# Two heads' first 64 queries in one softmax block: an attention and MoE kernel on one Trainium2 core

## Chip, core and metric

The kernel runs on one core of one Trainium2 chip. The metric is the time of one execution in device microseconds, taken as the median of several runs. TensorE is called PE here, VectorE DVE, ScalarE ACT, GpSimd POOL; SP is the engine that issues most DMAs. PEld is PE's loading of weights.

## What is computed

Causal attention over 2 batches, 12 heads, 448 positions, head size 64, and behind it two feed-forward parts:

```python
scores = scale * np.matmul(q, k.transpose(0, 1, 3, 2))
scores = np.where(mask, -1000000000.0, scores)       # mask: strictly above the diagonal
scores = scores - np.max(scores, axis=-1, keepdims=True)
attn = np.exp(scores)
attn = attn / (np.sum(attn, axis=-1, keepdims=True) + 1e-09)
x = np.matmul(attn, v)                               # then heads side by side: 896 x 768
h = (x @ w1) * (x @ w2) @ w3 @ w_out
r = np.maximum(h @ w_in2, 0.0)
out = (r * r) @ w_out2
```

## The kernel before

**Pairs and blocks.** The 24 heads are handled as 12 pairs; the two heads of a pair lie on partitions 0 to 63 and 64 to 127 of one tile `qk`. The 448 queries of a head are cut into four blocks of 128 rows (NCH = 4). Block i sees WIDTH[i] = 64 + 128 i keys: 64, 192, 320 and 448. Block 0 holds the first 64 queries on its upper 64 partitions; its lower 64 rows are the last 64 queries of the rolled tensor, carried along and never used. SHORT = 64 is that first width.

**One pair's steps.** `scores` (L668) has PE multiply queries by keys, for both heads in turn, into tiles `s`, two blocks to a tile in the order (3, 0), (2, 1). `minimum` (L709) has DVE apply the mask, write the block to tile `p` and take the row's extreme into `st`; each is followed by a short read of the accumulator. `softmax` (L715) has ACT exponentiate a block and sum its rows, DVE add 1e-9 and take reciprocals of four sums (`reciprocals`, L727, one call for each head), and DVE multiply each block by them. Then PE transposes: `short_transposes` (L763, tile `ph`) the blocks of 64 columns, eight for a pair, and `transposes` (L742, tile `pp`) the full ones. ACT copies both into `pt_all`; `attend` (L788, tile `x`) multiplies by the values, and `x_parts` splits the result for the products behind it.

**What lies between.** PE also forms w3 @ w_out during attention, in pieces called `w` (`fill`, `w_half`). From pair 4 on, one loop of the main program puts on PE: scores of pair p, `ph` of pair p-1, one `w`, the `pp`, two `w`, `x`. In the first loops PE does the scores of pairs 0 and 1, then 32 transposes of a constant (`warm`, L841), then `ph` of pair 0. From about 151 us on, PE works on the feed-forward products (tiles `bank`).

**Who sets the order.** Every step is entered in a `Program` (L28) with its engines, a cost on each and the places it reads and writes. PE's steps keep the order in which they are entered. For DVE, ACT and SP a list planner (`Program.order`, L59) works out due times backwards from PE's steps and gives each engine the ready step that is due first. The order is then fixed; each engine runs its list in order.

```python
mm(s_t[p, j, g][:, o:o + w], y[own, 0, rows_of(i):rows_of(i) + P], y[own, 1, :w], True, True)
prog.add({"V": (300, 380)}, reciprocals, sums, sums)
nc.tensor.transpose(x[0][:SHORT, o:o + SHORT], block(p, j, c)[SHORT:, c * P:c * P + SHORT], ident[SHORT:, SHORT:])
```

Of the kernel before, what the change touches and what calls it, by code (L numbers as in the profile page):

```python
# [8 lines left out]
F32 = mybir.dt.float32  # L9
F32R = mybir.dt.float32r  # L10
U32 = mybir.dt.uint32
AF = mybir.ActivationFunctionType
# [112 lines left out]
def attention_moe_moe2(ctx: ExitStack, tc: tile.TileContext, qk, v, w1, w2, w3, w_out, w_in2, w_out2, out):  # L125
# [48 lines left out]
    def mm(o, l, r, start, stop, **more):  # L174
        return nc.tensor.matmul(o, l, r, start=start, stop=stop, **more)  # L175
# [138 lines left out]
    for g in range(N3 // KF):  # L314
# [16 lines left out]
    wraw = [attw.tile([P, DM], F32, tag=f"W{i}", name=f"wraw{i}") for i in range(KF)]  # L331
    ident = attc.tile([P, P], F32, tag="ident", name="ident")
    mask = attc.tile([P, S], F32, tag="mask", name="mask")
    pt_all = attc.tile([P, 3, NCH * (SHORT + S) // 2], F32, tag="pt", name="pt_all")
    make_identity(nc, ident)
    nc.gpsimd.memset(mask, 0.0)
# [1 line left out]
        out=mask, in_=mask, compare_op=ALU.is_ge, fill=MASKED,  # L338
        base=S - P, pattern=[[-1, S]], channel_multiplier=1,
    )  # L340


    prog = Program({"S": 700, "V": 700})
# [319 lines left out]
        prog.add({"S": (700, 2900)}, run, [], [("v", p % 2)], turn="v")  # L663

    def place_p(p, j, i):
        return "p", (2 * p + j) % 4, i

    def scores(p):  # L668
        def open_tiles():
            st_t[p] = att.tile([P, 4, 2, NCH], F32, tag="st", name=f"st{p}", bufs=3)  # L670
            for h in (2 * p, 2 * p + 1):
                p_t[h] = att.tile([P, off[NCH]], F32, tag="p", name=f"p{h}", bufs=4)

        at = {}
        for g in BLOCKS:
            for j in range(2):
                at[j, g] = turn("a", 6)
        for g in BLOCKS:
            o = 0
            for i in g:  # L680
                w = WIDTH[i]

                def run(e, g=g, i=i, o=o, w=w):
                    if g == BLOCKS[0]:
# [8 lines left out]
                opened = [place_p(p, j, i2) for j in range(2) for i2 in range(NCH)] if g == BLOCKS[0] else []  # L693
                a = 3.3 if p == 0 and i == BLOCKS[0][0] else 1.856
                prog.add({"T": (a * w, a * w + 250)}, run, [("qk", p % 3)],
                         [("a", at[j, g]) for j in range(2)] + opened)
                o += w
        for j in range(2):
            for g in BLOCKS:
                o = 0  # L700
                for i in g:
                    w = WIDTH[i]
                    minimum(p, j, g, i, o, w, at[j, g])
                    o += w

    def block(p, j, i):
        return p_t[2 * p + j][:, off[i]:off[i + 1]]

    def minimum(p, j, g, i, o, w, place):  # L709
        gap = 80 + 1.031 * w  # L710
        prog.add({"V": (gap, gap + 160)}, lambda e: nc.vector.tensor_tensor_reduce(  # L711
            block(p, j, i), s_t[p, j, g][:, o:o + w], mask[:, S - w:], QS, 3.0e38,
            ALU.add, ALU.min, st_t[p][:, 0, j, i:i + 1]), [("a", place)], [place_p(p, j, i), ("st", p % 3, j, i)])

    def softmax(p, j):  # L715
        sums = []
        for g in BLOCKS:
            for i in g:
                w = WIDTH[i]
                gap = 272 + 0.882 * w  # L720
                prog.add({"A": (gap, gap + 100)}, lambda e, i=i: nc.scalar.activation(  # L721
                    block(p, j, i), block(p, j, i), AF.Exp, bias=st_t[p][:, 0, j, i:i + 1], scale=-1.0,
                    accum_out=st_t[p][:, 1, j, i:i + 1]),
                    [place_p(p, j, i), ("st", p % 3, j, i)], [place_p(p, j, i), ("st", p % 3, j, i)])
                sums.append(("st", p % 3, j, i))
# [6 lines left out]
        prog.add({"V": (300, 380)}, reciprocals, sums, sums)  # L732
        for g in BLOCKS:
            for i in g:
                w = WIDTH[i]
                on_v = 70 + 0.67 * w
                prog.add({"V": (on_v, on_v + 85)},
                         lambda e, i=i: nc.vector.tensor_scalar(  # L738
                             block(p, j, i), block(p, j, i), st_t[p][:, 3, j, i:i + 1], None, ALU.mult),
                         [place_p(p, j, i), ("st", p % 3, j, i)], [place_p(p, j, i)])  # L740

    def transposes(h):  # L742
        p, j = divmod(h, 2)
# [19 lines left out]
    def short_transposes(p):  # L763
        x, place = [], turn("a", 6)

        def run(e):
            x.append(ps_a.tile([P, S + SHORT], F32, tag="a", name=f"ph{p}"))
            for j in range(2):
                for c in range(NCH):
                    o = (j * NCH + HALF_AT[c]) * SHORT  # L770
                    nc.tensor.transpose(x[0][:SHORT, o:o + SHORT], block(p, j, c)[SHORT:, c * P:c * P + SHORT],
                                        ident[SHORT:, SHORT:])

        t = 2 * NCH * 56
        prog.add({"T": (t, t + 160)}, run, [place_p(p, j, i) for j in range(2) for i in range(NCH)], [("a", place)])
        for j in range(2):
            h = 2 * p + j

            for c, d in ((0, 1), (3, 2)):
                def out(e, j=j, h=h, c=c, d=d):  # L780
                    src = x[0][:SHORT, j * NCH * SHORT:(j + 1) * NCH * SHORT].rearrange("p (n c) -> p n c", c=SHORT)
# [682 lines left out]
```

## Time and profile before

| What | us |
|---|---|
| Median of 3 runs | 518.12 (516.83 to 518.4) |
| The profiled execution | 518.19 |
| its span, first to last instruction | 516.4 |
| DVE busy in the span | 478.6 |
| ACT busy in the span | 396.8 |

The profiled execution takes 1.8 us more than its span; that part lies around the instructions. Its granted clock is 0.999 of full speed. Times in the rows below count from the start of the span. A busy PE says little by itself: its matmuls are pipelined, the start of one lies before the end of the last, and their ends are modelled. The distance from start to start is what a matmul costs.

### The profile page before, as it was taken

The numbers are of one execution on the slowest core, as the hardware profiler recorded it, in microseconds if no ns is written. First come the engines' busy times: TensorE is split into PE (matmuls) and PEld (weight loads), VectorE is DVE, ScalarE is ACT, GpSimd is POOL, SyncE is SP. The second block draws the span as 40 slices with busy tenths as digits, with TensorE's granted clock in tenths as the row PEclk, the third lists the DMA queues.
The fourth block names the chain that finished last, engine by engine and source line by source line (L and its number), as shares of the span: only waits on it lengthen the run. The fifth ranks groups of instructions, "written<-read, shape, count | busy, mean of one in ns | idle before, by whom it ended". The sixth has DMA issues, their size and how long they took to land.

```text
span 516.4 us, 8564 instructions
## 1 busy us (share of the span) xinstructions
PE 510.5 (99%) x2915; PEld 464.5 (90%) x2915; DVE 478.6 (93%) x1147; ACT 396.8 (77%) x979; POOL 16.2 (3%) x24
## 2 busy tenths in 40 slices
PE   9999999999999999999999999999999999999997
PEld 7668888888889999999999999999999999999997
DVE  4999999999969999997976899999999999999994
ACT  5998999767859574638486479998999698969870
POOL 1000000000000012121100000000000000000000
PEclk9999999999999999999999999999999999999999
DMA  8955555563242887999754301505520642061014
GB/s 312 330 199 219 200 176 182 181 225 142 83 157 105 282 233 185 304 179 296 158 151 152 123 0 56 190 1 214 204 72 1 237 161 94 0 241 65 2 62 154
DMA packets 27340, 81.69 MB, mean 158 GB/s; under 512 B 2464, under 2 KB 13472, under 8 KB 27296
## 3 DMA queue, kind: packets, MB, share of 16 engines
q1 hardware_dynamic: 23520, 75.64, 41.7%
q0 software_dynamic: 3776, 5.51, 7.1%
q8 instruction: 23, 0.38, 0.3%
q14 instruction: 21, 0.17, 0.1%
HBM read 75.24 MB, written 14.55 MB: 174 GB/s over the span
## 4 chain that ended last, share of the span: by engine, by line
PE 80%; DVE 17%; ACT 1%; issue 0%; DVEq 0%
PE bank L175 70%; PE w L175 5%; DVE p L711 4%; DVE p L738 4%; DVE xs L511 2%; PE s L175 2%; PE x L175 2%; PE pp L753 1%; DVE w L434 1%; DVE fs L434 1%; DVE raw_w L507 1%; ACT p L721 1%; PE zeros L175 1%; DVE xB L434 1%; DVE st L730 1%; DVE wraw L434 1%
## 5 line engine op out<-in xcount | busy, mean ns | idle before, releaser
L441 ACT CAST ring<-xs 128x384 fp32r<-128x384 f32 (+1 forms) x194 | 104.1, 549 | 42.6 <-PE bank L175 26.7
L175 PE MATMUL bank<-xT,ring 128*128 128x448 f32 x630 | 132.0, 366 | 0.0
L175 PEld LDWEIGHTS bank<-xT,ring 128*128 128x128 f32 x630 | 117.9, 188 | 9.2
L434 DVE TENSOR_TENSOR ring<-xs,ring 128x384 fp32r<-128x384 f32 (+1 forms) x194 | 112.8, 591 | 11.6 <-ACT ring L441 11.4
L175 PE MATMUL bank<-ring,g 128*128 128x384 f32 x600 | 104.9, 335 | 0.0
L175 PEld LDWEIGHTS bank<-ring,g 128*128 128x128 f32 x600 | 104.2, 188 | 0.3 <-ACT bank L441 0.2
L175 PE MATMUL bank<-xB,ring 128*128 128x448 f32 x489 | 102.2, 366 | 0.0
L175 PEld LDWEIGHTS bank<-xB,ring 128*128 128x128 f32 x489 | 91.7, 188 | 7.4 <-ACT bank L441 0.2
L721 ACT ACTIVATE p<-p,st 128x320 f32<-128x320 f32 (+3 forms) x96 | 48.6, 527 | 11.3 <-DVE st L711 11.3
L434 DVE TENSOR_TENSOR xs<-xs 128x384 f32<-128x384 f32 x96 | 52.0, 554 | 0.1
L711 DVE CUSTOM_DVE_ANT_0 p<-s,mask 128x320 f32<-128x320 f32 (+3 forms) x96 | 34.7, 419 | 5.7 <-PE s L175 5.7
L434 DVE TENSOR_TENSOR g<-fs,g 128x384 fp32r<-128x384 f32 (+1 forms) x88 | 37.1, 433 | 0.5 <-ACT g L441 0.4
L175 PE MATMUL w<-hl_wout,w 128*128 128x384 f32 x192 | 36.2, 340 | 0.0
L441 ACT CAST g<-fs 128x384 fp32r<-128x384 f32 (+1 forms) x88 | 35.8, 426 | 0.1
L175 PEld LDWEIGHTS w<-hl_wout,w 128*128 128x128 f32 x192 | 33.0, 188 | 0.5
L441 ACT COPY fs<-bank 128x448 f32<-128x448 f32 (+1 forms) x52 | 27.4, 529 | 6.7 <-PE bank L175 6.5
L175 PE MATMUL bank<-ab,ring 128*128 128x448 f32 x144 | 29.5, 365 | 0.0
L175 PEld LDWEIGHTS bank<-ab,ring 128*128 128x128 f32 x144 | 27.1, 188 | 2.1
L503 ACT ACTIVATE xs<-raw_w 128x768 f32<-128x768 f32 (+1 forms) x30 | 24.1, 823 | 5.3 <-DVE w L434 1.7
L175 PE MATMUL w<-ring,w 128*128 128x384 f32 x144 | 27.4, 342 | 0.0
L738 DVE TENSOR_SCALAR p<-p,st 128x448 f32<-128x448 f32 (+3 forms) x96 | 26.6, 346 | 0.0
L434 DVE TENSOR_TENSOR fs<-bank,fs 128x448 f32<-128x448 f32 x41 | 25.5, 622 | 1.1 <-PE bank L175 1.1
(87 smaller groups left out, 688.9 us busy)
## 6 DMA issues: line engine op xcount, KB each, us to landing
raw_wout<-in_w_out SPq DMA_DIRECT2D x20, 768.0 KB, 4.8
raw_w<-in_w SPq DMA_DIRECT2D x16, 768.0 KB, 6.0
raw_win<-in_w_in SPq DMA_DIRECT2D x16, 768.0 KB, 5.0
raw_w<-in_w SPq DMA_DIRECT2D x16, 512.0 KB, 4.5
qk<-in_qk SPq DMA_DIRECT2D x12, 448.0 KB, 5.3
s_dram<-w_dram POOLq DMA_DIRECT2D x8, 576.0 KB, 9.0
v<-in_v SPq DMA_DIRECT2D x12, 256.0 KB, 2.8
raw_wout<-in_w_out SPq DMA_DIRECT2D x8, 384.0 KB, 8.0
```

Source lines behind the costliest of these rows:

```text
L175: return nc.tensor.matmul(o, l, r, start=start, stop=stop, **more)
L434: return lambda e: engine_of[e].tensor_tensor(out(), x(), y(), op=what)
L441: return lambda e: engine_of[e].copy(out(), x()) if e == "A" else engine_of[e].tensor_copy(out(), x())
L503: nc.scalar.activation(y(), raws[key][:, cols, 1].bitcast(F32), AF.Prelu, scale=2.0 ** -112, alpha=-2.0 ** 32)
L507: nc.vector.tensor_scalar(x, x, 2.0 ** -29, 7.0, ALU.mult, ALU.min)
L511: nc.vector.scalar_tensor_tensor(yi, yi, 3, raws[key][:, cols, 0], op0=ALU.logical_shift_left, op1=ALU.bitwise_or)
L711: prog.add({"V": (gap, gap + 160)}, lambda e: nc.vector.tensor_tensor_reduce(block(p, j, i), s_t[p, j, g][:, o:o + w], mask[:, S - w:], QS ...
L721: prog.add({"A": (gap, gap + 100)}, lambda e, i=i: nc.scalar.activation(block(p, j, i), block(p, j, i), AF.Exp, bias=st_t[p][:, 0, j, i:i ...
L730: nc.vector.reciprocal(st[:, 3], st[:, 2])
L738: lambda e, i=i: nc.vector.tensor_scalar(block(p, j, i), block(p, j, i), st_t[p][:, 3, j, i:i + 1], None, ALU.mult),
L753: nc.tensor.transpose(x[0][:, o:o + P], block(p, j, i)[:, c * P:(c + 1) * P], ident)
```

## The change

The first 64 queries of the pair's two heads now share one block of 128 rows: head 0 on partitions 0 to 63, head 1 on 64 to 127. It has a tile of its own (`p0`), a mask of its own (`mask0`, made by POOL at the start) and one place in `st`, which now holds 7 sums of a pair in place of 8. So a pair has 7 blocks in softmax: 7 minima, 7 exponentials, 7 multiplications. The two matmuls that make this block use 64 columns of queries each, and write to the lower and upper half of the partitions of one tile `s`. Of the eight transposes of 64 x 64, two become one of 128 x 64. From pair 1 on, one call takes the reciprocals of all 7 sums of the pair, so that no block is multiplied before the last exponential of both heads; pair 0 keeps a call for each head.

```diff
+    mask0 = attc.tile([P, SHORT], F32, tag="mask0", name="mask0")
...
+    nc.gpsimd.memset(mask0, 0.0)
+    for j in range(2):
+        nc.gpsimd.affine_select(
...
     def place_p(p, j, i):
-        return "p", (2 * p + j) % 4, i
+        return ("p", (2 * p + j) % 4, i) if i else ("p0", p % 2)
+
+    def stat(j, i):
+        return i + (NCH - 1) * j if i else 0
+
+    def blocks_of(j):
+        return [i for g in BLOCKS for i in g if i or j == 0]
...
-                        mm(s_t[p, j, g][:, o:o + w], y[own, 0, rows_of(i):rows_of(i) + P], y[own, 1, :w], True, True)
...
+                        if i:
+                            mm(s_t[p, j, g][:, o:o + w], y[own, 0, rows_of(i):rows_of(i) + P], y[own, 1, :w],
+                               True, True)
+                        else:
+                            mm(s_t[p, 0, g][j * SHORT:(j + 1) * SHORT, o:o + w], y[own, 0, S - SHORT:],
+                               y[own, 1, :w], True, True)
...
-                    minimum(p, j, g, i, o, w, at[j, g])
+                    if i or j == 0:
+                        minimum(p, j, g, i, o, w, at[j, g])
...
-    def softmax(p, j):
+    def softmax(p, heads):
...
         def reciprocals(e):
-            st = st_t[p][:, :, j]
+            st = st_t[p][:, :, min(sums):max(sums) + 1]
             nc.vector.tensor_scalar(st[:, 2], st[:, 1], 1.0e-9, None, ALU.add)
             nc.vector.reciprocal(st[:, 3], st[:, 2])
...
+            nc.tensor.transpose(x[0][:SHORT, :2 * SHORT], p0_t[p], ident)
             for j in range(2):
-                for c in range(NCH):
-                    o = (j * NCH + HALF_AT[c]) * SHORT
+                for c in range(1, NCH):
+                    o = (2 * HALF_AT[c] + j) * SHORT
...
-            for j in range(2):
-                softmax(p, j)
+            for heads in ((0,), (1,)) if p == 0 else ((0, 1),):
+                softmax(p, heads)
```

On PE the steps keep their order and change their shapes. This is PE at the scores of pair 2 and the short transposes of pair 1, before; in a name such as `s_0_3` the first number is the head and the second the first block in the tile, the last number only counts tiles, and `p_173`, `p_174` are the two heads' blocks of pair 1:

```order
L175 MATMUL s_0_3_337<-qk_141 128x448
L175 MATMUL s_1_3_339<-qk_141 128x448
L175 MATMUL s_0_3_337<-qk_141 128x64
L175 MATMUL s_1_3_339<-qk_141 128x64
L175 MATMUL s_0_2_355<-qk_141 128x320
L175 MATMUL s_1_2_357<-qk_141 128x320
L175 MATMUL s_0_2_355<-qk_141 128x192
L175 MATMUL s_1_2_357<-qk_141 128x192
L771 MATMUL ph_365<-ident,p_173 64x64 x4
L771 MATMUL ph_365<-ident,p_174 64x64 x4
L175 MATMUL w_0_379<-xs,w_0_271 128x384 x4
```

And now (`p_1_165` is the shared block of pair 1):

```order
L175 MATMUL s_0_3_333<-qk_150 128x448
L175 MATMUL s_1_3_335<-qk_150 128x448
L175 MATMUL s_0_3_333<-qk_150 64x64 x2
L175 MATMUL s_0_2_347<-qk_150 128x320
L175 MATMUL s_1_2_349<-qk_150 128x320
L175 MATMUL s_0_2_347<-qk_150 128x192
L175 MATMUL s_1_2_349<-qk_150 128x192
L792 MATMUL ph_359<-ident,p_1_165 64x128
L796 MATMUL ph_359<-ident,p_166 64x64 x3
L796 MATMUL ph_359<-ident,p_167 64x64 x3
L175 MATMUL w_0_376<-xs,w_0_259 128x384 x4
```

The two 64-wide score matmuls write 64 partitions each where they wrote 128, and a transpose that reads all 128 partitions stands between the scores and the six transposes that read 64.

This is DVE at the second head's reciprocals and multiplications of pair 1, before; the first head's four multiplications stand further ahead in its list:

```order
L729 TENSOR_SCALAR st_172<-st_172 128x4
L730 RECIPROCAL st_172<-st_172 128x4
L511 SCALAR_TENSOR_TENSOR xs<-xs,raw_wout_166 128x384
L738 TENSOR_SCALAR p_174<-p_174,st_172 128x448
L738 TENSOR_SCALAR p_174<-p_174,st_172 128x320
L738 TENSOR_SCALAR p_174<-p_174,st_172 128x192
L738 TENSOR_SCALAR p_174<-p_174,st_172 128x64
```

And now:

```order
L752 TENSOR_SCALAR st_164<-st_164 128x7
L753 RECIPROCAL st_164<-st_164 128x7
L518 SCALAR_TENSOR_TENSOR xs<-xs,raw_wout_173 128x384
L762 TENSOR_SCALAR p_166<-p_166,st_164 128x448
L762 TENSOR_SCALAR p_167<-p_167,st_164 128x448
L762 TENSOR_SCALAR p_166<-p_166,st_164 128x320
L762 TENSOR_SCALAR p_167<-p_167,st_164 128x320
L762 TENSOR_SCALAR p_166<-p_166,st_164 128x192
L762 TENSOR_SCALAR p_167<-p_167,st_164 128x192
L762 TENSOR_SCALAR p_1_165<-p_1_165,st_164 128x64
```

Seven multiplications stand behind the pair's last exponential where four stood. SP's list changes too: from its 26th entry on, some loads of weights, of `qk` and of `v` and some stores of `w` change places.

## Rows read from the trace of the kernel before

**Rows 1.** The page, busy us (share of the span) and instructions.

```profile
PE 510.5 (99%) x2915; PEld 464.5 (90%) x2915; DVE 478.6 (93%) x1147; ACT 396.8 (77%) x979; POOL 16.2 (3%) x24
```

**Rows 2.** What PE waited for, whole span: us in total, times, longest.

```profile
PE ph L771 <- DVE p L738: 1.2, 2, 1.0
```

**Rows 3.** Timeline of PE, one period: start us, length us, what, count.

```profile
67.28 2.11 PE L175 MATMUL s<-qk 64*128 64x448 f32 x16
69.23 0.61 PE L771 MATMUL ph<-ident,p 64*64 64x64 f32 x8
...
79.43 2.11 PE L175 MATMUL s<-qk 64*128 64x448 f32 x16
```

**Rows 4.** The chain that ended last: start us, us, what.

```profile
31.75 0.45 PE ph L771 x8
...
49.13 2.12 PE w L175 x12
...
150.78 361.02 PE bank L175 x1871
```

**Rows 5.** The same chain: one 64-wide minimum, two 64-wide multiplications on DVE.

```profile
10.77 0.14 DVE p L711
...
79.35 0.33 DVE p L738 x2
```

**Rows 6.** Timeline of PE, end of attend and start of scores.

```profile
67.12 0.22 PE L175 MATMUL x<-pt_all,v 128*64 128x64 f32 x1
67.28 0.65 PE L175 MATMUL s<-qk 64*128 64x448 f32 x2
...
67.76 0.54 PE L175 MATMUL s<-qk 64*128 64x448 f32 x2
```

**Rows 7.** Timeline of PE, within those scores.

```profile
68.13 0.66 PE L175 MATMUL s<-qk 64*128 64x64 f32 x6
...
68.62 0.44 PE L175 MATMUL s<-qk 64*128 64x320 f32 x2
```

**Rows 8.** Timeline of PE, end of a `w` and start of attend.

```profile
65.13 0.34 PE L175 MATMUL w<-ring,w 128*128 128x384 f32 x1
...
65.40 0.60 PE L175 MATMUL x<-pt_all,v 128*64 128x448 f32 x2
...
65.82 0.55 PE L175 MATMUL x<-pt_all,v 128*64 128x448 f32 x2
```

**Rows 9.** Timeline of PE, end of scores and start of short transposes.

```profile
69.06 0.32 PE L175 MATMUL s<-qk 64*128 64x192 f32 x1
69.23 0.33 PE L771 MATMUL ph<-ident,p 64*64 64x64 f32 x3
```

**Rows 10.** Timeline of PE, end of pair 1's scores and start of `warm`.

```profile
9.18 0.33 PE L175 MATMUL s<-qk 64*128 64x192 f32 x2
9.44 0.33 PE L847 MATMUL warm<-ident 128*128 128x128 f32 x1
...
9.60 0.38 PE L847 MATMUL warm<-ident 128*128 128x128 f32 x2
```

**Rows 11.** Timeline of PE, all of `warm`, then pair 0's short transposes.

```profile
9.44 3.71 PE L847 MATMUL warm<-ident 128*128 128x128 f32 x32
14.13 0.63 PE L771 MATMUL ph<-ident,p 64*64 64x64 f32 x8 [0.99 <-DVE p L738]
```

**Rows 12.** Timeline of DVE and of PE, pair 1: multiplications, short transposes.

```profile
19.37 1.14 DVE L738 TENSOR_SCALAR p<-p,st 128x448 f32<-128x448 f32 x4
...
20.55 0.61 PE L771 MATMUL ph<-ident,p 64*64 64x64 f32 x8
```

**Rows 13.** The same, pair 3.

```profile
42.76 1.14 DVE L738 TENSOR_SCALAR p<-p,st 128x448 f32<-128x448 f32 x4
...
44.91 0.61 PE L771 MATMUL ph<-ident,p 64*64 64x64 f32 x8
```

**Rows 14.** Timeline of PE, pair 11's short transposes.

```profile
140.51 0.60 PE L771 MATMUL ph<-ident,p 64*64 64x64 f32 x8 [0.24 <-DVE p L738]
```

More of the change, by code (lines that the diff above doesn't have):

```diff
@@ L340, in attention_moe_moe2 @@
     )
+    nc.gpsimd.memset(mask0, 0.0)
+    for j in range(2):
+        nc.gpsimd.affine_select(
+            out=mask0[j * SHORT:(j + 1) * SHORT], in_=mask0[j * SHORT:(j + 1) * SHORT], compare_op=ALU.is_ge,
+            fill=MASKED, base=0, pattern=[[-1, SHORT]], channel_multiplier=1,
+        )
     prog = Program({"S": 700, "V": 700})
@@ L665, in place_p @@
     def place_p(p, j, i):
-        return "p", (2 * p + j) % 4, i
+        return ("p", (2 * p + j) % 4, i) if i else ("p0", p % 2)
[3 more added lines that the diff above has]
+        return [i for g in BLOCKS for i in g if i or j == 0]
     def scores(p):
         def open_tiles():
-            st_t[p] = att.tile([P, 4, 2, NCH], F32, tag="st", name=f"st{p}", bufs=3)
+            st_t[p] = att.tile([P, 4, 2 * NCH - 1], F32, tag="st", name=f"st{p}", bufs=3)
+            p0_t[p] = att.tile([P, SHORT], F32, tag="p0", name=f"p0_{p}")
             for h in (2 * p, 2 * p + 1):
-                p_t[h] = att.tile([P, off[NCH]], F32, tag="p", name=f"p{h}", bufs=4)
+                p_t[h] = att.tile([P, off[NCH] - SHORT], F32, tag="p", name=f"p{h}", bufs=4)
         at = {}
@@ L683, in run @@
                 def run(e, g=g, i=i, o=o, w=w):
-                    if g == BLOCKS[0]:
+                    if g == BLOCKS[0] and o == 0:
                         open_tiles()
@@ L690, in run @@
                         own = slice(j * D, (j + 1) * D)
-                        mm(s_t[p, j, g][:, o:o + w], y[own, 0, rows_of(i):rows_of(i) + P], y[own, 1, :w], True, True)
-                opened = [place_p(p, j, i2) for j in range(2) for i2 in range(NCH)] if g == BLOCKS[0] else []
+                        if i:
[4 more added lines that the diff above has]
+                               y[own, 1, :w], True, True)
+                opened = [place_p(p, j, i2) for j in range(2) for i2 in range(j, NCH)] if g == BLOCKS[0] else []
                 a = 3.3 if p == 0 and i == BLOCKS[0][0] else 1.856
                 prog.add({"T": (a * w, a * w + 250)}, run, [("qk", p % 3)],
-                         [("a", at[j, g]) for j in range(2)] + opened)
+                         [("a", at[j, g]) for j in range(2 if i else 1)] + opened)
                 o += w
@@ L702, in scores @@
                     w = WIDTH[i]
-                    minimum(p, j, g, i, o, w, at[j, g])
+                    if i or j == 0:
+                        minimum(p, j, g, i, o, w, at[j, g])
                     o += w
+    p0_t = {}
     def block(p, j, i):
-        return p_t[2 * p + j][:, off[i]:off[i + 1]]
+        return p_t[2 * p + j][:, off[i] - SHORT:off[i + 1] - SHORT] if i else p0_t[p]
     def minimum(p, j, g, i, o, w, place):
@@ L711, in minimum @@
         prog.add({"V": (gap, gap + 160)}, lambda e: nc.vector.tensor_tensor_reduce(
-            block(p, j, i), s_t[p, j, g][:, o:o + w], mask[:, S - w:], QS, 3.0e38,
-            ALU.add, ALU.min, st_t[p][:, 0, j, i:i + 1]), [("a", place)], [place_p(p, j, i), ("st", p % 3, j, i)])
-    def softmax(p, j):
+            block(p, j, i), s_t[p, j, g][:, o:o + w], mask[:, S - w:] if i else mask0, QS, 3.0e38,
+            ALU.add, ALU.min, st_t[p][:, 0, stat(j, i):stat(j, i) + 1]),
+            [("a", place)], [place_p(p, j, i), ("st", p % 3, stat(j, i))])
@@ L716, in softmax @@
+    def softmax(p, heads):
         sums = []
-        for g in BLOCKS:
-            for i in g:
-                w = WIDTH[i]
+        for j in heads:
+            for i in blocks_of(j):
+                w, k = WIDTH[i], stat(j, i)
                 gap = 272 + 0.882 * w
[L721 to L725, printed above, removed]
+                names = [place_p(p, j, i), ("st", p % 3, k)]
+                prog.add({"A": (gap, gap + 100)}, lambda e, j=j, i=i, k=k: nc.scalar.activation(
+                    block(p, j, i), block(p, j, i), AF.Exp, bias=st_t[p][:, 0, k:k + 1], scale=-1.0,
+                    accum_out=st_t[p][:, 1, k:k + 1]), names, names)
+                sums.append(k)
@@ L727, in reciprocals @@
         def reciprocals(e):
-            st = st_t[p][:, :, j]
+            st = st_t[p][:, :, min(sums):max(sums) + 1]
             nc.vector.tensor_scalar(st[:, 2], st[:, 1], 1.0e-9, None, ALU.add)
             nc.vector.reciprocal(st[:, 3], st[:, 2])
[L732 to L735, printed above, removed]
+        names = [("st", p % 3, k) for k in sums]
+        prog.add({"V": (300, 380)}, reciprocals, names, names)
@@ L736, in softmax @@
+        for j in heads:
+            for i in blocks_of(j):
+                w, k = WIDTH[i], stat(j, i)
                 on_v = 70 + 0.67 * w
                 prog.add({"V": (on_v, on_v + 85)},
-                         lambda e, i=i: nc.vector.tensor_scalar(
-                             block(p, j, i), block(p, j, i), st_t[p][:, 3, j, i:i + 1], None, ALU.mult),
-                         [place_p(p, j, i), ("st", p % 3, j, i)], [place_p(p, j, i)])
+                         lambda e, j=j, i=i, k=k: nc.vector.tensor_scalar(
+                             block(p, j, i), block(p, j, i), st_t[p][:, 3, k:k + 1], None, ALU.mult),
+                         [place_p(p, j, i), ("st", p % 3, k)], [place_p(p, j, i)])
@@ L780, in out @@
                 def out(e, j=j, h=h, c=c, d=d):
[L781 removed]
+                    src = x[0][:SHORT].rearrange("p (n i c) -> p n i c", i=2, c=SHORT)[:, :, j]
                     dst = pt_all[:SHORT, h % 3].rearrange("p (n c) -> p n c", c=SHORT)
```

## The prediction

> **What bounds the kernel now.** The page comes first: PE is busy for 99% of the span and DVE for 93% [rows 1], so either could be the limit of attention, and a change that lightens DVE would pay only if it is DVE. The list of waits decides: in the whole span PE waits for DVE twice, 1.2 us in all, and for ACT or a DMA never [rows 2]. The timeline says the same: from the scores of one pair to those of the next PE takes 79.43 - 67.28 = 12.15 us, one matmul behind the other [rows 3]. The chain of waits walks through DVE for most of attention, but that is a chain followed back from one tie at its end, a wait of 0.24 us [rows 14]; DVE is full there and hardly ever late. Behind attention PE runs 361.02 us in one piece [rows 4]. So the end moves by what PE's own instructions get longer or shorter, and by its two waits.
>
> **Prices on PE.** In a shape like 64*128 the numbers are the rows and columns of the array that a matmul's weights take. A pass with 448 moving columns takes 68.13 - 67.76 = 0.37 us start to start [rows 6, 7], so one with 64 takes 0.053 and one with 192 takes 0.16. A `w` matmul takes 2.12 / 12 = 0.177 and a short transpose 0.45 / 8 = 0.056 [rows 4].
>
> Where the shape of the weights changes, PE loses time twice: the first pass starts late, and lasts longer, since its weights were not loaded ahead.
> - 128*64 to 64*128: the start is 0.16 - 0.053 = 0.10 late, the first pass 0.48 in place of 0.37 [rows 6]. Together 0.21.
> - 128*128 to 128*64: the start is 0.27 - 0.177 = 0.09 late, the first pass 0.42 in place of 0.37 [rows 8]. Together 0.14.
> - 64*128 to a transpose with 128*128: the start is 0.26 - 0.16 = 0.10 late [rows 10], the first transpose takes 0.16 in place of about 0.11, which is (3.71 - 0.33) / 31 [rows 10, 11]. Together 0.15.
> - 64*128 to short transposes with 64*64: 0.17 against 0.16 [rows 9]. Nothing is lost.
>
> So rows are split over whether every change of shape is paid for, and this is the open question of the forecast. The Trainium skill's page "TensorEngine Tiling", section "Key Properties", says that changing the tiling mode, not merely the tile, drains TensorE; by that rule all four are paid, and the sum is the one below; by rows 9 alone it would be rival 1's. The trace agrees with it in three and disagrees in the fourth. The same page, section "Restrictions", sets column tiling against transposes of fp32 data, by which the fourth would be no change of columns at all; no run here shows that.
>
> **Scores.** Before, all blocks have weights of 64*128. The narrow block and the pass behind it (64, 64 and 320 columns, 448 in all) take 68.62 - 68.13 = 0.49 us where 0.37 would do [rows 7]: 0.12 is lost to weights of 128 columns that load longer than 64 columns stream. Now the narrow block has 64*64 and stands between blocks of 64*128. If both edges are paid, the way in costs 0.14 (columns 128 to 64, and a load of 64 columns, as in rows 8) and the way out 0.21 (a load of 128, as in rows 6), and the 0.12 is contained in them: 0.37 + 0.14 + 0.21 = 0.72, which is 0.23 more. If neither is paid, 0.12 is gained. I take +0.23, since three of four edges in the trace are paid and the free one leads to transposes, which these are not. For ten pairs (2 to 11) that is +2.3 us; ends -1.2 and +2.3. Pairs 0 and 1 come before `warm`, where PE waits for DVE in any case.
>
> **Short transposes.** Eight of 0.056 become six and one of about 0.11: no difference. But the scores (64 rows) are now followed by a transpose with 128*64, and that by six with 64*64. The first edge changes 64 rows to 128 as in rows 10: +0.15, where nothing was lost before [rows 9]. The second changes 128 rows to 64: 0.10 as in rows 6, and at most 0.05 for the load, which I take half of: +0.12. The edge to `w` behind them stays. Together some +0.25 for a pair, +2.5 us for pairs 1 to 10; ends 0 (if transposes never pay) and +3.1 (both edges as in rows 10).
>
> **Start and end.** Pair 0's short transposes wait 0.99 us for DVE [rows 11], whose list ahead of them gets shorter by two 64-wide minima of 0.14 (pairs 0 and 1) and one multiplication of 0.33 / 2 [rows 5]: -0.45 us. PE is free in time: `warm` ends at about 13.1 and its start moves by two narrow blocks. The edge within the short transposes adds 0.12. At pair 11 the wait of 0.24 us goes [rows 14], since DVE has less to do and PE is later, and the same edge adds 0.12; attend before it has 128*64 as well, so there is no other. Together -0.33 and -0.12.
>
> **The merged reciprocals.** In pair 1 the second head's four multiplications begin at 19.37 and take 1.14 us; the short transposes start at 20.55, hardly later [rows 12]. Now all seven stand behind the last exponential. Three more, of 448, 320 and 192 columns, are about 1.14 - 0.165 = 0.9 more. What comes before them on DVE and ACT is some 0.3 earlier, and so is PE, which then loses that again in the scores: a wait of about 0.5, of which 0.1 hides the edge: +0.4 us; ends 0 and +0.9. In pair 3 the room is 44.91 - 43.90 = 1.0 us [rows 13], just enough, and PE comes later by then.
>
> **Costed at nothing.** Per pair DVE loses a minimum, a multiplication and one set of reciprocals, ACT one exponential. Neither is waited for, so this is room and no gain. POOL makes the new mask ahead of the third minimum; it has 24 instructions in the whole span [rows 1], and if it were late it would only eat the 0.45 of the start. SP's loads change places by an entry or two; PE waited for no load [rows 2], and the queries have three buffers. If that cover went, scores would be seen to wait for `qk`. DVE's and ACT's own lists are reordered up to the end of attention, in which PE's list is unchanged.
>
> **Sum.** 2.3 + 2.5 - 0.33 - 0.12 + 0.4 = 4.75 us. The profiled execution took 518.19 us (span 516.4, and 1.8 around it), 0.07 over the median; 518.19 + 4.75 = 522.9 us.
>
> **Rivals.**
> 1. *Edges within 64 rows are free* in the scores, in both directions, as into the short transposes [rows 9]. Then scores gain 1.2, transposes still lose 2.5, the rest is -0.05: +1.25, 519.4 us, no measurable change. It decides at the narrow block: at under 0.4 us for it and the next pass this holds. For it speaks one of four edges; against it, that the columns' change alone is paid in rows 8.
> 2. *Free into the narrow block, paid out of it*: 0.37 + 0.21 - 0.49 = +0.09 a pair, 0.9 + 2.5 - 0.05 = +3.35: 521.5 us.
> 3. *The two heads' narrow matmuls run one after the other.* They ran side by side and wrote two tiles; now they write two halves of the partitions of one tile from two halves of the rows. Two passes of 0.053 for ten pairs are 1.1 more: 524.0 us. Against it: attend writes halves of one tile side by side (the two that start at 65.40 [rows 8]), though from the same rows. The Trainium skill's page "TensorEngine Tiling", section "Gotcha 1: PSUM Pressure", says that different row tiles cannot access one PSUM bank at once, which is this case; no row of the trace before has it.
> 4. *No new edge is paid.* If also the two around the new transpose run like rows 9, PE gains 1.2 in the scores and 0.45 + 0.24 in its waits, less 0.4 at pair 1: -1.5, 516.7 us, faster by about 0.3%. Against it stand rows 6 and 10, which change rows and pay.
> 5. *Every pair waits as pair 1 does*, because seven multiplications come late: ten times 0.4 more, 526.9 us. Against it: pair 3's room, and a PE that takes some 0.5 us longer per pair while DVE has less to do.
>
> **How the numbers follow.** Forecast 0.56 (its own range 522.0 to 523.7, by the loads' shares), rival 1 0.14, rival 2 0.14, rival 3 0.08, rival 4 0.04, rival 5 0.04. The range 519.2 to 524.3 takes in the forecast and rivals 1 to 3. About 0.3%, 1.55 us, can be told from no change. Rival 4 lies at the edge of faster; with runs that spread by 1.6 us I give 0.06. Rival 1 lies within 0.3%, though near its upper edge: 0.12. Slower: 0.82.
>
> **What would show it.** In the timeline after, PE's period from scores to scores should be about 12.6 us; the last 448-wide pass to the second 320-wide one, start to start, 1.09 (now 0.86 [rows 6, 7]); scores to first short transpose 0.26 and the whole set of short transposes 0.25 longer; the `bank` stretch should begin at about 155.5 and still last 361 us. DVE should show idle time in attention. I am wrong if the period stays at 12.15 with both edges there, if PE waits for DVE more than at pair 0 and pair 1, or if the `bank` stretch changes its length.

## The result, and the profile after

The changed kernel takes 523.44 us (median of 6 runs, 522.72 to 525.38), the kernel before 518.67 in the runs beside it. The ratio is 1.0103, with a 95% interval of 1.0078 to 1.0128: slower by about 1%. The forecast was 522.9 us, in a range of 519.2 to 524.3, and slower with a chance of 0.82. The profiled execution took 522.74 us (span 521.0), 4.55 more than that of before; the sum had 4.75.

The page after, busy time by engine, and the list of what PE waited for (us in total, times, longest):

```profile
PE 515.8 (99%) x2903; PEld 462.0 (89%) x2903; DVE 473.5 (91%) x1088; ACT 395.1 (76%) x956; POOL 16.7 (3%) x27
```

```profile
PE zeros L175 <- DVE xs L857: 1.1, 1, 1.1
PE ph L792 <- DVE p L762: 0.5, 1, 0.5
```

DVE has 5.1 us less to do than before [rows 1], ACT 1.7, and PE 5.3 more. The 1.2 us for which PE waited at the short transposes [rows 2] have become 0.5. So the work that the change was to save was saved, on engines for which PE hardly waits, and PE paid. (The wait at `zeros` is one of 1.1 us in the first microsecond; the kernel before has it too.)

The timeline of PE, one period of attention (start us, length us, what, count; a row gathers matmuls that follow one another, under the name of its first):

```profile
69.41 2.35 PE L175 MATMUL s<-qk 64*128 64x448 f32 x16
71.68 0.30 PE L792 MATMUL ph<-ident,p 128*64 128x128 f32 x1
71.91 0.52 PE L796 MATMUL ph<-ident,p 64*64 64x64 f32 x6
72.36 2.38 PE L175 MATMUL w<-ring,w 128*128 128x384 f32 x12
...
82.04 0.65 PE L175 MATMUL s<-qk 64*128 64x448 f32 x2
```

From scores to scores it is 82.04 - 69.41 = 12.63 us, where it was 12.15 [rows 3]: 0.48 more, in two places. The scores take 2.35 in place of 2.11. And from the start of the first short transpose to the first `w` it is now 72.36 - 71.68 = 0.68, for what was 0.54 in the trace of before, with another 0.09 lost just ahead of it. The same view, cut smaller, within these scores:

```profile
69.89 0.80 PE L175 MATMUL s<-qk 64*128 64x448 f32 x6
...
70.36 0.33 PE L175 MATMUL s<-qk 64*64 64x64 f32 x4
...
70.46 0.69 PE L175 MATMUL s<-qk 64*64 64x64 f32 x4
...
70.62 0.54 PE L175 MATMUL s<-qk 64*128 64x320 f32 x2
...
70.99 0.44 PE L175 MATMUL s<-qk 64*128 64x320 f32 x2
```

From the last 448-wide pass to the narrow block it is 70.36 - 69.89 = 0.47, where a pass takes 0.37: 0.10 lost. The narrow block's own passes start at 70.357 and 70.464 in the trace, the 320 block's at 70.619 and 70.992: 0.05 lost in the first narrow pass, 0.10 on the way out, 0.11 in the first 320-wide pass (0.27 would do). From the last 448-wide pass to the second 320-wide one that makes 1.11 us. Before it was 0.87 by the trace's nanoseconds, 0.86 by the rounded rows [rows 6, 7]; the forecast had 1.09. The narrow matmuls of the two heads start 0.006 us apart: they run side by side.

The start, PE's timeline of pairs 0 and 1, and ScalarE's between them:

```profile
13.79 0.30 PE L792 MATMUL ph<-ident,p 128*64 128x128 f32 x1 [0.54 <-DVE p L762]
...
15.93 2.95 PE L175 MATMUL x<-pt_all,v 128*64 128x448 f32 x16
18.81 2.35 PE L175 MATMUL s<-qk 64*128 64x448 f32 x16
21.09 0.30 PE L792 MATMUL ph<-ident,p 128*64 128x128 f32 x1
```

```profile
14.73 0.24 ACT L809 COPY pt_all<-ph 64x128 f32<-64x128 f32 x1
15.16 1.41 ACT L783 COPY pt_all<-pp 128x384 f32<-128x384 f32 x4 [0.19 <-PE pp L777]
16.46 0.59 ACT L809 COPY pt_all<-ph 64x128 f32<-64x128 f32 x3
```

Pair 0's short transposes start at 13.79, 0.34 earlier [rows 11]. Pair 1's wait for nothing; DVE's last multiplication for them ends 0.30 us ahead. But the attention matmuls of pair 0 take 18.81 - 15.93 = 2.88 us. ScalarE copies three of the four parts of `ph` only at 16.46, behind four copies of the wide transposes, and head 1's first attention matmul follows at 16.94, when head 0, which started at 15.93, is through its first block. So for a while one head runs alone.

In the kernel before, the same matmuls took 18.60 - 16.16 = 2.44 us; PE's timeline, and ScalarE's:

```profile
16.16 2.51 PE L175 MATMUL x<-pt_all,v 128*64 128x448 f32 x16
18.60 2.11 PE L175 MATMUL s<-qk 64*128 64x448 f32 x16
```

```profile
15.39 0.76 ACT L759 COPY pt_all<-pp 128x384 f32<-128x384 f32 x2 [0.17 <-PE pp L753]
16.03 0.26 ACT L784 COPY pt_all<-ph 64x128 f32<-64x128 f32 x1
16.19 0.75 ACT L759 COPY pt_all<-pp 128x384 f32<-128x384 f32 x2
```

There short and wide copies took turns. Head 1 was late even so: it started at 16.73 in the trace, 0.57 behind head 0, when the first of its wide copies was done. With the change it is 1.01 behind, and the difference is the 0.44. The list of waits shows neither, because the other head keeps PE busy meanwhile.

The chain of waits (start us, us, what) ends as it did [rows 4], 4.84 us later and 0.24 shorter:

```profile
155.62 360.78 PE bank L175 x1871
```

### The profile page after: what moved, and what is told of

The parts are those of the page before. It is cut to its first block, busy times and chain, and to the rows that moved or that the text cites. A ratio compares the mean times of both kernels' runs of the same rounds, so it can differ in the third digit from the quotient of the medians.

```text
span 521.0 us, 8479 instructions
## 1 busy us (share of the span) xinstructions
PE 515.8 (99%) x2903; PEld 462.0 (89%) x2903; DVE 473.5 (91%) x1088; ACT 395.1 (76%) x956; POOL 16.7 (3%) x27
## 4 chain that ended last, share of the span: by engine, by line
PE 98%; DVE 2%; issue 0%; DVEq 0%
PE bank L175 69%; PE w L175 14%; PE s L175 5%; PE x L175 5%; PE pp L777 3%; PE ph L796 1%; DVE p L733 1%; PE zeros L175 1%; PE ph L792 1%; DVE p L762 0%; DVE g L441 0%; DVE st L753 0%; DVE xs L857 0%; DVE st L752 0%; DVE st L733 0%
## 5 line engine op out<-in xcount | busy, mean ns | idle before, releaser
L745 ACT ACTIVATE p<-p,st 128x320 f32<-128x320 f32 (+3 forms) x84 | 44.2, 540 | 11.7 <-DVE st L733 11.7
L733 DVE CUSTOM_DVE_ANT_0 p<-s,mask 128x320 f32<-128x320 f32 (+3 forms) x84 | 32.7, 446 | 5.6 <-PE s L175 5.6
L175 PE MATMUL s<-qk 64*128 64x448 f32 (+3 forms) x192 | 28.7, 417 | 0.0
```

Of the source, the lines that this page charges most:

```text
L745: prog.add({"A": (gap, gap + 100)}, lambda e, j=j, i=i, k=k: nc.scalar.activation(block(p, j, i), block(p, j, i), AF.Exp, bias=st_t[p][:, ...
```

## The experiments

For each kernel: the ratio to the kernel before, which ran beside it (the change itself has 1.0103), the usual period of attention (before 12.15, the change 12.63), and the start of the first `bank` matmul (150.71 and 155.55). That start is of one execution each: the time from pair 0's scores to pair 1's, ahead of most of what the edits touch, was between 2.58 and 3.20 us in the five traces (the change, e2_early, e4_split, e5_swap, e10_act) whose PE lists are alike up to there.

| kernel | median us | ratio, 95% | period | `bank` |
|---|---|---|---|---|
| e1_wide | 521.06 | 1.0053 (1.0027 to 1.0078) | 12.39 | 153.73 |
| e2_early | 522.02 | 1.0064 (1.0039 to 1.0089) | 12.53 | 154.26 |
| e7_both | 520.98 | 1.0046 (1.0029 to 1.0064) | 12.27 | 151.61 |
| e4_split | 522.86 | 1.0089 (1.0064 to 1.0115) | 12.63 | 155.72 |
| e5_swap | 520.37 | 1.0039 (1.0020 to 1.0058) | 12.31 | 152.00 |
| e6_one | 527.00 | 1.0176 (1.0145 to 1.0207) | 12.86 | 157.97 |
| e8_all | 520.74 | 1.0058 (1.0038 to 1.0079) | 12.08 | 152.95 |
| e9_diag | 518.08 | 0.9996 (0.9980 to 1.0013) | 12.01 | 150.74 |
| e10_act | 522.46 | 1.0088 (1.0058 to 1.0119) | 12.63 | 154.69 |
| e11_split | 518.36 | 0.9997 (0.9976 to 1.0019) | 12.01 | 150.37 |

**Undo the edges in the scores.** e1_wide:

```
-    mm(s_t[p, 0, g][j * SHORT:(j + 1) * SHORT, o:o + w], y[own, 0, S - SHORT:],
+    f = y.rearrange("p i s -> p (i s)")
+    mm(s_t[p, j, g][:, o:o + w], f[own, S - (1 + j) * SHORT:S + (1 - j) * SHORT],
```

> The change, with its narrow score matmuls as they were before it: for each head 64 rows by 128 columns of weights (the last 64 of those columns hold other queries or keys and fill rows that nobody reads), each head in its own tile; the minimum reads the two halves in two instructions (one more on DVE for each pair, about 0.17 us). Everything else of the change stays. Theory (edges): the scores lose the two changes of tiling and go back from 2.43 to 2.19 us for each pair (narrow block to 320 block 1.11 back to 0.87 us), so the attention stage is 10 x 0.24 = 2.4 us shorter than with the change: 523.4 becomes about 521.0. PE stays without waits, because DVE still has 2 us of margin ahead of the short transposes. Rival (DVE or the order of the work costs the time, and the edges are hidden beside other waits): removing the edges gives nothing, 523.4, or a little more for the added minimum. Rival (serialised heads): the same time as the theory, but the two heads' narrow matmuls of the change would have to start one after the other in its trace, which they don't.

521.06 us. Two scores in PE's timeline:

```profile
56.43 2.11 PE L175 MATMUL s<-qk 64*128 64x448 f32 x16
...
68.82 0.65 PE L175 MATMUL s<-qk 64*128 64x448 f32 x2
```

The scores are back at 2.11 us and the period is 12.39, 0.24 under the change. One of the seven periods from pair 4 on is 0.19 us longer, at an attention matmul that waits for ScalarE's `w`. At pair 0 PE waits 1.4 us for DVE, 0.9 more than with the change, and its short transposes start 0.38 later: DVE has a minimum more for each of pairs 0 and 1. That is why `bank` starts 1.8 us earlier and not 2.4. The theory holds for this half, and the rival that edges are hidden falls.

**Undo the edges at the short transposes, first try.** e2_early moves the shared block's transpose behind the attention matmuls of the pair two before:

```
+        if p > 2:
+            first_transpose(p - 1)
         if p < NP_ALL:
             load_pair(p)
```

> The change, with the one transpose of the shared block (64 columns of weights over 128 rows) moved ahead: from pair 2 on it stands directly behind the attention matmuls of the pair two before, which have the same 128 x 64 weights, and no longer between the scores (64 rows) and the short transposes (64 rows). Nothing else changes. Theory (edges): the pass from the scores to what follows falls from 0.93 back to about 0.70 us where no new edge is made, that is for pairs 2 and 4 to 10 (8 of them); at pair 3 a 128 x 128 matmul group stands between, so the edge only moves; pairs 0, 1 and 11 are as with the change. 8 x 0.235 = 1.9 us less: about 521.5. The transpose itself is then seen 0.16 us behind the last attention matmul. Rival (the edge is paid anyway where the tiling goes from 128 to 64 rows next to it): 523.4. Rival (the multiplication of the shared block isn't done by then, so PE waits for DVE about 2 us ahead of the old place): waits of PE for the tile p at the new place, and 523.4 or more.

522.02 us against 521.5: the period falls by 0.10 only, not by 0.235. PE's timeline at the new place:

```profile
68.48 0.28 PE L175 MATMUL x<-pt_all,v 128*64 128x64 f32 x4
68.69 0.30 PE L794 MATMUL ph<-ident,p 128*64 128x128 f32 x1
68.92 0.64 PE L175 MATMUL s<-qk 64*128 64x448 f32 x1
```

Four attention passes (two heads side by side, 0.056 apart) stand ahead of the transpose, so it should begin at about 68.60 if 128*64 followed on 128*64 without loss. It begins at 68.69, with 0.10 lost, as at a change of shape. No wait for the tile `p` shows, and the second rival falls. (At pair 0, where nothing was to change, all four copies of `ph` now stand behind four wide ones, and PE waits 0.8 us at the attention matmuls.) What the expectation had wrong is that two operations with the same numbers in the trace have the same tiling.

**Both undone in this way.** e7_both is e1_wide with that move.

> Both: narrow scores with 128 columns of weights as before the change, and the shared block's transpose ahead, behind the attention matmuls. What is left of the change is one exponential, one multiplication and one minimum pair on a shared block, one 128 row transpose in place of two 64 row ones, and the merged reciprocals. Theory (edges): 523.4 - 2.4 - 1.9 = 519.1, less about 0.1 for each pair by the transposes that fall away from the short group (one transpose of 128 rows in place of two: two of 55 ns against 107 ns, so nothing), plus the 0.44 at attend of pair 0 that stays: 518.5 to 519.3, about the time of the kernel before. Rival (DVE's share bounds the attention stage): with 0.85 us less DVE work for each pair than before and no edges, 8 us less than before, about 510. Rival (the loss is not in the edges): 523.4.

520.98 us, too slow by some 2, and not in the way of the rivals either. Its usual period of 12.27 is what the two runs apart give (12.63 - 0.24 - 0.10 = 12.29). In the trace `bank` starts 3.94 us earlier than with the change, for most of which ten periods of 0.36 account, although PE waits at pair 0 (the first two rows below), where ScalarE's copies are late as with the change. But behind attention the `bank` stretch takes 1.5 longer; 0.4 of that is a wait for ACT (the third row), and the rest has no cause that was shown:

```profile
PE ph L800 <- DVE p L768: 1.0, 1, 1.0
PE x L175 <- issue: 0.8, 1, 0.8
PE bank L175 <- ACT bank L448: 0.4, 1, 0.4
```

DVE's lighter load shows no gain: with 12.27 the period is still over the 12.15 of before.

**The second half of the change alone taken back.** e4_split:

```
-            for heads in ((0,), (1,)) if p == 0 else ((0, 1),):
+            for heads in ((0,), (1,)):
```

> The change without its second half: from pair 1 on the reciprocals come for each head by itself, as in pair 0 (one more small pair of instructions on DVE for each pair, and head 0's multiplications ahead of head 1's exponentials). Theory (edges): PE doesn't wait for DVE after the change except once at pair 0, so the order on DVE is off the path: no difference, within 0.4 us of 523.4. The late start of head 1 in the attention matmuls of pair 0 (2.88 us in place of 2.44) stays, since ScalarE's copies there stand in the same order. Rival (the merged reciprocals hold back head 0's multiplications and so the short transposes): 1 to 4 us less, and before this run the trace of the change would show PE waiting for the tile p in several pairs.

522.86 us, the same waits of PE, the same period: within these intervals the merged reciprocals cost nothing and give nothing here. (The planner puts DVE's and ACT's lists in another order for it, behind pair 0's short transposes; ACT's copies at pair 0 stay in theirs.)

**Which 64s make an edge.** Two runs put the question that e2_early left. e5_swap moves the shared block's transpose to the end of its group, between 64 rows and 128 rows, where an edge is paid anyway:

```
-            nc.tensor.transpose(x[0][:SHORT, :2 * SHORT], p0_t[p], ident)
             for j in range(2):
...
+            nc.tensor.transpose(x[0][:SHORT, :2 * SHORT], p0_t[p], ident)
```

> The change with one line moved: the transpose of the shared block comes last of the seven short transposes, not first, so that it stands between the 64 row transposes and the 128 row matmuls that follow (w, or the wide transposes), and no longer between two groups of 64 rows. Theory A (a transpose with 64 columns of weights runs at the full width of the array, so its tiling differs from its neighbours by its rows alone; the matmuls of the attention, which fill two column halves side by side, differ from it): scores to short transposes go back to 0.16 us without an edge, the edge from 64 to 128 rows that was paid ahead of w is now paid ahead of the shared block's transpose, and that one to w is free: last score pass to first w 0.70 us again in place of 0.93, in every pair: 11 x 0.234 = 2.6 us less than the change, about 520.8. Theory B (64 and 128 columns of weights always differ, also for transposes): a new edge of about 0.1 us between that transpose and w, so only half of it, about 522.1. Rival (edges are not what is paid): 523.4.

520.37 us. PE's timeline:

```profile
69.98 0.33 PE L175 MATMUL s<-qk 64*128 64x192 f32 x2
70.15 0.49 PE L795 MATMUL ph<-ident,p 64*64 64x64 f32 x6
70.58 0.30 PE L797 MATMUL ph<-ident,p 128*64 128x128 f32 x1
70.63 0.59 PE L175 MATMUL w<-ring,w 128*128 128x384 f32 x2
```

The scores' last pass is followed after 0.17 us, with nothing lost, as before the change [rows 9], and `w` starts 0.05 us behind the transpose: from a transpose with 128*64 to a matmul with 128*128 there is no edge. That is theory A, and somewhat more than it asked, 0.32 a period in place of 0.234: the transpose, 0.11 by itself, delays `w` by 0.05. The profiled execution took 521.61 us, near the longest of ten (518.36 to 521.74): from the first `bank` matmul to the end of the span it lasts 367.84 us in place of 365.42, because 600 matmuls from 213 us on took 123.5 us in place of 121.2, at a granted clock of 1.00 in both; no cause for it was found in the kernel.

e6_one leaves head 0's narrow matmul at 64 columns, in partitions 0 to 63, and gives head 1 128:

```
-    mm(s_t[p, j, g][:, o:o + w], f[own, S - (1 + j) * SHORT:S + (1 - j) * SHORT],
+    mm(s_t[p, j, g][:P if j else SHORT, o:o + w], f[own, S - (1 + j) * SHORT:S],
```

(the first line is that of e1_wide)

> As the run with wide narrow scores (128 columns of weights for each head, own tile), but head 0 alone uses 64 columns of weights again: its 64 queries go to the first 64 partitions, where a full-width matmul would put them as well. Head 1 keeps 128 columns. Theory A (what makes the edge is a column half of its own, that is an output that begins at partition 64): no edge, last 448 pass to last-but-one 320 pass 0.87 us as in the kernel before, 521.1 in all. Theory B (64 columns of weights in a matmul make the edge wherever they stand): 1.0 to 1.1 us there, and 522 to 523.4 in all.

527.00 us (four runs, 525.14 to 529.4): theory B, but above its 523.4, and worse than the change. PE's timeline:

```profile
70.44 2.56 PE L175 MATMUL s<-qk 64*128 64x448 f32 x16
...
71.39 0.33 PE L175 MATMUL s<-qk 64*64 64x64 f32 x2
...
71.64 0.54 PE L175 MATMUL s<-qk 64*128 64x64 f32 x2
```

The scores take 2.56 us. Head 0's two passes stand alone from 71.39, and head 1's first begins only at 71.64: with different tilings the heads' narrow blocks no longer run side by side. So a matmul with 64 columns of weights makes an edge also in the first partitions; a transpose with 64 does not.

**ScalarE's order at pair 0.** e10_act puts the wide copies of pair 0 behind the short ones:

```
-                    [("a", place)], [("pt", h % 3, c)])
+                    [("a", place)], [("pt", h % 3, c)], behind=short_copies if p == 0 else [])
...
-                prog.add(act(2 * SHORT, True), out, [("a", place)], [("pt", h % 3, "h", c)])
+                short_copies.append(prog.add(act(2 * SHORT, True), out, [("a", place)], [("pt", h % 3, "h", c)]))
```

> The change, with one thing forced: ScalarE makes the four copies of pair 0's short transposes ahead of the six of its wide transposes (in the change one of the four stands ahead, three behind four of the wide ones). Theory (the attention matmuls of pair 0 are long because head 1 waits for such a copy): those matmuls, first to last, fall from 2.88 us to 2.44 or to the time that the next copy sets, not under 2.4; 0.2 to 0.45 us less in all, 523.0 to 523.2, and the first matmul of the bank stretch at 155.1 to 155.35 us in place of 155.55. Rival (the two heads' matmuls there are slow for another reason, as the tiling): 2.88 us and 155.55 as with the change.

522.46 us; the difference to the change is too small for the times, so the trace decides. PE's timeline:

```profile
13.36 0.30 PE L792 MATMUL ph<-ident,p 128*64 128x128 f32 x1 [0.54 <-DVE p L762]
...
15.51 2.35 PE L175 MATMUL x<-pt_all,v 128*64 128x448 f32 x16
17.79 2.35 PE L175 MATMUL s<-qk 64*128 64x448 f32 x16
20.22 0.30 PE L792 MATMUL ph<-ident,p 128*64 128x128 f32 x1
```

The attention matmuls of pair 0 take 17.79 - 15.51 = 2.28 us, 0.60 less than with the change and, against what was expected, less than 2.44. From pair 0's short transposes to pair 1's it is 6.86 in place of 7.30 us, with a wait of 0.08 for DVE in it. (In this execution pair 0's first scores took 0.4 us less, ahead of all that the edit touches; so its `bank` starts 0.86 earlier, not 0.43.)

**All repairs.** e8_all is e1_wide, e5_swap and e10_act in one.

> Three repairs together: wide narrow scores, the shared block's transpose last of the short ones, and ScalarE's four copies of pair 0's short transposes ahead of its six wide ones, so that the attention matmuls of pair 0 find both heads ready (2.88 back to 2.44 us). Theory (the edges in the scores, the edges at the short transposes and the copies' order are all that the change costs): 523.4 - 2.3 - 2.6 - 0.4 = 518.1, the time of the kernel before within 0.5; first matmul of the bank stretch at 150.5 to 151.2 us (155.55 with the change, 150.71 before). Rival (with these gone, DVE's lighter load shows as speed): 516 or less. Rival (some cost of the change is not among the three): 519.5 or more.

520.74 us, 2.6 over the forecast, as the second rival had it (519.5 or more). Undisturbed periods take 12.08 us, less than before the change. But PE now waits for ACT and DVE in the middle of attention, more than in any kernel above:

```profile
PE ph L801 <- DVE p L768: 1.0, 1, 1.0
PE w L175 <- ACT wraw L448: 0.6, 1, 0.6
PE x L175 <- ACT w L448: 0.5, 1, 0.5
PE w L175 <- DVE xB L441: 0.5, 1, 0.5
PE x L175 <- issue: 0.4, 1, 0.4
```

The first and the last line are at pair 0. The other three, 1.6 us, are in three later loops, and the periods at two of them last 1.0 and 0.7 us longer than 12.08. PE is faster by 0.55 a pair than with the change, and it seems that the two engines that had room have none left in single pairs; no run here shows that as the cause.

**Another form of the narrow scores.** e9_diag makes them one matmul with both heads' queries on the diagonal of a zeroed tile, ahead of attention (with e5_swap and e10_act):

```
+    prog.add({"P": (300, 400)}, lambda e, own=own: nc.gpsimd.tensor_copy(
+        qz[own, p % 3, own], qk_t[p][own, 0, S - SHORT:]), [("qk", p % 3)], [("qz", p % 3, j)])
...
+    mm(s_t[p, 0, BLOCKS[0]][:, S:], qz[:, p % 3], qk_t[p][:, 1, :SHORT], True, True)
```

> The last, with another form of the narrow scores: both heads' first 64 queries stand as two blocks on the diagonal of a zeroed 128 x 128 tile (two 64 x 64 copies by POOL for each pair), so that one matmul over all 128 rows with 128 columns of weights gives the shared block whole, for one minimum of DVE; from pair 2 on it stands ahead of the attention matmuls, behind matmuls or transposes of the same 128 x 128 tiling, and so makes no edge of its own. Theory (edges and passes are what PE is paid for): two passes of about 0.055 us in place of two of 0.107, 0.1 us less for each pair than in the last run, 1.0 to 1.3 us in all: 516.8 to 517.1 if that one comes out at 518.1, faster than the kernel before by 0.2%. Rival (a wait for POOL's copies or for the scores' bank, taken earlier now, eats it): PE waits at that matmul, 518.1 or more. Rival (the stretch after the attention stage can't take work earlier, because DVE and ScalarE feed it): the bank stretch begins earlier, but lasts that much longer.

518.08 us, 1.0 over a forecast that hung on 518.1 for e8_all; it is 2.7 under what e8_all came to, and no different from the kernel before. PE's timeline:

```profile
65.19 0.33 PE L175 MATMUL s<-qk,qz 128*128 128x64 f32 x2
65.45 1.95 PE L175 MATMUL x<-pt_all,v 128*64 128x448 f32 x16
67.33 1.89 PE L175 MATMUL s<-qk 64*128 64x448 f32 x12
...
79.35 1.89 PE L175 MATMUL s<-qk 64*128 64x448 f32 x12
...
20.86 0.35 PE L824 MATMUL ph<-ident,p 64*64 64x64 f32 x3 [0.84 <-DVE p L791]
...
140.23 0.47 PE L824 MATMUL ph<-ident,p 64*64 64x64 f32 x4 [0.30 <-DVE p L791]
```

The period is 79.35 - 67.33 = 12.02, 0.13 under the kernel before, and the new matmul waits for nothing. Over ten pairs that is 1.3 us, but it goes back: 0.84 in a wait for DVE at pair 1, 0.30 in one at pair 11, and one period, behind a `w` that waits for DVE, is 0.65 longer. With one minimum less for each pair than e8_all it has hardly any of that kernel's other waits; how much of those was load and how much the order that the planner gave ACT and DVE was not separated.

**The same with reciprocals by head.** e11_split is e9_diag with the edit of e4_split.

> The last repaired kernel (block-diagonal narrow scores, transpose of the shared block last, copies in order), without the second half of the change: reciprocals for each head by itself in every pair. That kernel still waits for DVE at the short transposes of pair 1 (0.84 us) and pair 11 (0.30 us). Theory (the merged reciprocals wait for the exponentials of both heads, and all seven multiplications stand behind them): head 0's multiplications start earlier, the wait at pair 11 goes, that at pair 1 falls by up to half; 0.3 to 0.7 us less, 517.4 to 517.8. Rival (ScalarE ends both heads' exponentials one right behind the other, so that merging costs nothing, and the two added small instructions cost DVE about 0.2 us for each pair): the same waits, 518.1.

518.36 us against 517.4 to 517.8, ratio 0.9997: no difference. The wait at pair 1 shrinks to 0.19 and that at pair 11 to 0.08, as the theory said, but other waits for ACT and DVE come up, the longest this one:

```profile
PE x L175 <- ACT w L450: 0.4, 1, 0.4
```

No kernel here is measurably faster than the one before the change.

## Why the prediction was right, and where it was not

- **What bounds the kernel.** Right. PE was the limit by the list of waits, against the page's 93% for DVE and the chain's walk through DVE. The change took 5.1 us from DVE, and the kernel became slower by about what was added to PE. e7_both, which leaves DVE light, is no faster than the kernel before. Two readings were too short. PE waits for DVE a third time, 1.1 us at `zeros`; both kernels do, so nothing hung on it. And that PE never waited for ACT holds for the list of waits alone, as pair 0 shows.
- **The edges in the scores.** Forecast +0.23 a pair, measured 1.11 - 0.87 = +0.24, and e1_wide takes them back. Rivals 1 and 2 (edges free, or free on one side) fall with the narrow rows above: both sides are paid, 0.10 for each change and another 0.05 and 0.11 in the first pass behind it.
- **The edges at the short transposes.** Forecast +0.25 (its two terms, 0.15 and 0.12, make 0.27), measured +0.234 from the scores' last pass to the first `w`; e5_swap takes them back. Rival 4 falls.
- **Rows 9.** The prediction left open why 64*128 to 64*64 was free there and took the free edge for something that transposes do. That was right, and e2_early, e5_swap and e6_one say more exactly what: the 64*64 of a transpose is not the 64*64 of a matmul. Where the rows are the same, a transpose of 64 columns follows matmuls of 128 columns, and is followed by them, without loss, and pays behind matmuls of 64. This is as if it ran at full width. The Trainium skill's page "TensorEngine Tiling", section "Restrictions", lists the transpose mode for fp32 input among what column tiling disables. The runs agree with it: 0.17 us into the transposes in e5_swap, a plain pass. The same page of the Trainium skill, section "Key Properties", says that a change of the tiling mode drains TensorE, and not a mere change of tile. The runs agree with that too, once the transposes are counted as full width: each change of rows or columns looked at above cost about 0.1 us ahead of the first pass, and two heads on two tiles of one shape start 0.006 us apart.
- **The two heads in one bank.** Rival 3 falls: the two heads' narrow matmuls write two halves of the partitions of one tile `s`, and so of one bank, from two halves of the rows, and start 0.006 us apart, as they did with a tile each. The Trainium skill's page "TensorEngine Tiling", section "Gotcha 1: PSUM Pressure", says that different row tiles cannot use one PSUM bank at once. The trace disagrees for this case: where two heads do run one after the other, in e6_one, the second starts 0.25 us late.
- **The start and pair 11.** The wait at pair 0 fell by the forecast 0.45, to 0.54, but what counts is the start of the transposes, and that came 0.34 earlier and not 0.45: DVE was ready 0.34 earlier, and the rest is `warm`, which began 0.10 later. The 0.24 at pair 11 went.
- **The step that failed: "The merged reciprocals", "a wait of about 0.5 ... +0.4" at pair 1.** The size came out by luck, the cause did not. There is no wait at pair 1's short transposes, so this term was 0. Pair 0's attention matmuls take 0.44 us longer, because ScalarE makes three of the four short copies behind four wide ones; e10_act, which changes that order alone, takes it back, and e4_split, which takes the merging back, does not. The prediction read that ACT's list is reordered and costed this at nothing, since PE had never waited for ACT in the list of waits. At pair 0 that room was none: the matmuls of before, 2.44 us in place of the usual 1.88, were already late on ACT's copies.
- **The sum.** In the trace of after, `bank` starts 4.84 us later and its chain is 0.24 us shorter: 4.6 us, where 4.75 were forecast. Without the 0.44 us at pair 0, which the forecast did not have, it would be 4.2; the edges, 2.4 and 2.3 us, carry the sum. Rival 5 falls: no pair behind pair 0 waits.

## What to carry to other kernels

When several engines are 90% busy, look at what the full one waits for before giving another one less to do; work saved on an engine that is hardly ever late was worth next to nothing here, and the price of its new layout on PE was paid in full. Cost a change on PE by the shapes of neighbours in its list: a group of another tiling put between two equal ones costs two edges, here 0.24 us for a block of 64 columns, while the same group placed where the tiling changes anyway costs next to nothing (e5_swap moved one line for 0.32 us a pair). Do not take a list of waits for all lateness: with two heads side by side, one can be late while the other keeps PE busy. And where a planner orders ACT's list, look at the copies' order at the few places where PE is already close behind them.

## What was not expected of the hardware

- A transpose and a matmul with the same shape of weights in the trace behaved as two tilings: 128*64 behind 128*64 lost 0.10 us in e2_early, and 128*64 ahead of 128*128 lost nothing in e5_swap.
- Two heads in two halves of the rows, which run side by side with equal shapes, ran one after the other in the block in which one had 64 columns of weights and the other 128 (71.39 and 71.64 us in e6_one).
- 600 matmuls of one execution took 2% longer than the same ones in another (123.5 and 121.2 us), with the granted clock at 1.00 in both records.
